# One ramp for three masks, two merged first loads and a new start of the instruction lists, in an attention and SwiGLU kernel

## The chip, the cores and the metric

The kernel runs on one core of a Trainium2 chip. The metric is the device time of one execution in microseconds (us); three runs of the kernel before are shown, and one profiled execution. Engines are named as the profile names them: PE is TensorE (PEld its weight loads), DVE is VectorE, ACT is ScalarE, POOL is GpSimd, SP is SyncE.

## The reference

Attention with 16 extra "beacon" keys for each head, then a SwiGLU feed-forward block over all 4608 tokens (8 batches of 576). There are 8 heads of 64, d_model is 512 and d_ff 1536.

```python
k_all = np.concatenate([beacon_k, k], axis=2)        # 16 + 576 keys
v_all = np.concatenate([beacon_v, v], axis=2)
scores = scale * np.matmul(q, k_all.transpose(0, 1, 3, 2))
scores = np.where(causal, -1000000000.0, scores)     # the beacons are always seen
a = exp(scores - max); a /= a.sum(-1, keepdims=True) + 1e-09
x = np.matmul(a, v_all), heads side by side: 4608 x 512
g = x @ w_gate
out = (g * (1 / (1 + np.exp(-g))) * (x @ w_val)) @ w_out
```

## The kernel before, in words

**Attention.** Heads are worked in pairs (m = 0 to 3), one on the upper and one on the lower 64 rows of PE. The scores of a pair are cut into four units, A to D (`UNITS`); batch 0 runs them in the order of `FIRST_UNITS`: A0 A1 A2 A3, then B0 C0 D0, B1 C1 D1 and so on. A unit takes one PSUM slot of two banks, four slots in all (`take`, `give`). `scores` writes it, `exponent` (ACT, line 414) turns it into bf16 probabilities, `pv` multiplies with the values, `normalize` (DVE) divides. A causal diagonal is masked in one of two ways: in PE, with matmuls that add `ident` times `below` (line 404, plan letter `s`), or after the exponent, by DVE with `upper` (line 423) or by an `affine_select` on POOL (line 427).

**Queries and keys of batch 0** are loaded with their rows on partitions (`runs`, line 216), rows 0 to 255 of each head first (`FRONT`), the rest later. PE transposes them in five turns (`turn`): turn 0 is head pair 0 and turn 1 pair 1 and turn 2 pairs 2 and 3 for the first rows; turn 3 is pairs 0 and 1 and turn 4 pairs 2 and 3 for the rest. `turned_copy` (plan letters K and Q on DVE, k and q on ACT) copies each result to `kT` and `qT`. The first rows of heads 0 and 1 come through `first`, on the SP and ACT queues; all other loads are issued by POOL. Batches 1 and 2 are re-ordered by `pair_up` into `side` first, on DVE or POOL, and then turned (turn 5 is batch 1, pair 0).

**Feed-forward.** `gate_value` (letters G and H) makes 18 units for chunk 0 (units of 240 and 272 tokens, then of 512), later 12 for each chunk of 512 tokens; unit n needs columns 128 f to 128 f + 127 of both weights, `wg` and `wv`, which come in five parts each (g0 to g4, u0 to u4 in the list of loads; f = 3 to 5 is in part 2). `tanh` (ACT), `act1` and `act2` (DVE) follow, then `project` (F) and `evacuate` (O on DVE, o on ACT), which copies a bank of 128 tokens to SBUF and stores it.

**Order.** Nothing is scheduled by a tool: `plan` is a string with one letter for each step, and each engine runs its part of it in that order. `order_of_loads` lists the loads that letters L and l issue; at most eight POOL transfers are under way, a ninth waits for the first of them. Waits between engines are placed by the framework wherever two instructions touch the same tile; `apart` declares that two do not conflict, and is used where two banks of one PSUM tile are handled by different engines:

```python
ins = copy(eng, o_sb[:, cols], ps[:, at, cols])
apart(ins, copied.get((key, 1 - at), []))
```

The last 256 tokens are projected in two parts of 320 and 192 columns, each in a bank of its own (`PARTS`), so that part 0 is copied out beside the matmuls of part 1. `warm` and `keep_warm` (letter h) are matmuls without a use, in places where PE waits.

Of the kernel before, what the change touches and what calls it, by code (L numbers as in the profile page):

```python
# [85 lines left out]
def kernel(  # L86
# [591 lines left out]
    nc.vector.memset(pt[2][:, 0, 0:TOK], 0.0)  # L678
    nc.vector.memset(ident[:], 0.0)
    nc.vector.memset(below[:], 0.0)  # L680
    nc.vector.memset(upper[:], 1.0)
# [7 lines left out]
    def select_below():  # L689
        for row in range(2):  # L690
            r = slice(HALF * row, HALF * row + HALF)
            nc.gpsimd.affine_select(  # L692
                out=below[r], in_=below[r], compare_op=ALU.is_ge, fill=-30000.0, base=0,
                pattern=[[HALF, 2], [-1, P]], channel_multiplier=1,
            )

    def select_upper():
        nc.gpsimd.affine_select(
            out=upper[:], in_=upper[:], compare_op=ALU.is_ge, fill=0.0, base=0, pattern=[[1, P + NB]],
            channel_multiplier=-1,  # L700
        )
# [12 lines left out]
    for b in range(1, NPE):  # L714
        nc.vector.memset(beacons[b][:], 0.0)
    for i in range(NPT):
        nc.vector.memset(pt[i][:, :, 1664:P_W], 0.0)
    for i in range(2):
# [3 lines left out]


# [30 lines left out]
    def piece(kind):  # L754
# [17 lines left out]
        elif kind == "B":  # L772
            select_below()
        elif kind == "U":
            select_upper()
# [57 lines left out]
    ll2ltGHal1G2lGHHa1aatlt21tGH1H2lattF2aGFH112FF2FFGSaEFlHt1GFFaHa2Gltl1t2GtlH12latH12Fa12FFGGtDHS
    ltlaE1FHFFaG2lSFHtl12allF12GFElMFllFHaSG1FEFHaGFFolMHl2l1G2aSOF1H2FaE1FtFG2sHFEaFslF1FDFlSE2FDFE
    DFSESlPpFFFRlDFFFlStFESSDFFEFFsEDFOPEpMPEOpSFFlFRMStRFEFEFSsFEMEFFDFFPplFSFFFFFlFRDSSEFEtFtSFDFF
    FFFEEFlVFFsoOElFFSFtFFDFtSMPEDEtSFElpSDRFFMFFtlMPtESSFEEpRFttFFGFDDSEGHFGa12HHlla1aG21FHl2aGlFHl
    1a2GSHD1ool2aDtPlEGM1ltp2HRlla1GtlSlGH2alEGHG1l2FaM1HHF2a1GFa2HS1FF2FSFFaEFSFEF12lFSPEFpDMFEFSlS
    RFFlEFFtSFttEFFDFSFVFFESEtFFFMsMDEFFFDFEsOFSFFolPttDEFDFSpFFEMFsESFRFFFEFFtFPMEGGOtHoSEtaplHRPtl
    a11Gpt2HD2tGMRaGSt1HH2tGEa1al2G1HSa2GEH1a2GttHGa12SHH1a2MEG1GaM2DSHHES12FaEFFFFF1FDla2FFPSF1FE2F
    pRFFSFFSEFSFESFFFFVEFSFFFFDDFEFFEFFDSoFPFFMlFpFEStlFERFFFFFSSDoEPMFFEFFFDDOMGpoRSElPHGa1S2pHEaR1  # L840
    G2sHlGGEDaHaD12GG1Ha2H12aG1Ha2HaGG12S1EHlHGa2a1D2MSH1FEl2GSMFa1H2EMPaFDF1FSF2EDFFFpSFEFFsRFFFSFF
    FSEFPEEFFSFpERFFSFFFMDVFMSFFDEEPFFDSoFFFFpFFFFEFDOFSPRFDFSpEGFFFEGRGDDFHaO1oHH2aa12P1GpRHGGH2VaG
    Ha1a12HG2Ga1H122HGa1Ga2G1HHH2aa1a21G21GH2aG12HaHGFFFF1a2FFGF1H2aHaGF1H2FaF1GF2F1GHHFFFaa2FF12G1G
    HaFFFFH12F2FFFFFFaG1FHFFoFaFoFF212GGFHaFF1FHFF2FFaFGFFFFOHoG12GHHFaa12GFaFFF1FFF21FHF2GGFFaHFaFF
    1FFF12FHa2FG1GFHF2HFaF1FoaFFoFFFFFG2FF1FFHFaF1FGFF2HGFFFaFF12FH2FFaFFFFF1FFFFF2oFFFFFFFFFFFFOFFF
    FFFFOFoFFFFFFFFFFFOoFFFFFFOo
# [43 lines left out]
```

## Time and profile before

| what | value |
|---|---|
| three runs | 363.02, 363.58, 364.44 us (median 363.58) |
| the profiled execution | 364.1 us, of which the span is 362.1 us |
| TensorE | 352.4 us busy, 97% of the span |
| VectorE, ScalarE, GpSimd | 223.8, 188.9, 124.8 us busy |
| granted TensorE clock | 1.00 throughout |

The span runs from the first to the last instruction; 2.0 us of the profiled execution lie outside it. An engine's busy time leaves out waits, register and semaphore instructions. A time in a row is counted from the start of the span.

### The profile page before, as it was taken

How to read it: one execution, taken by the hardware profiler on the slowest of the kernel's cores; microseconds unless marked ns; L12 is line 12 of the kernel's file. 1: busy time of each engine (PE TensorE's matmuls, PEld its weight loads, DVE VectorE, ACT ScalarE, POOL GpSimd, SP SyncE). 2: the span in 40 equal slices, each digit the busy share in tenths (PEclk: the TensorE clock that was granted, in tenths of full speed). 3: DMA queues.
4: the chain of work that ended last, by engine and by line, in shares of the span. 5: the costliest groups of instructions: out<-in, count | busy, mean ns of one | idle time of the engine just before them, and what ended most of it. 6: DMA issues, size and time to landing. Idle time of an engine off the chain costs nothing.

```text
span 362.1 us, 11881 instructions
## 1 busy us (share of the span) xinstructions
PE 352.4 (97%) x5160; PEld 199.0 (55%) x5160; DVE 223.8 (62%) x437; ACT 188.9 (52%) x286; POOL 124.8 (34%) x188
## 2 busy tenths in 40 slices
PE   7789999999999999999999999999999999999996
PEld 3577566654444565544565556545655554455554
DVE  5576987667765753487518763777467764464341
ACT  4965999832425677543864466546633332331311
POOL 8953589936337545285423013112000000000000
PEclk9999999999999999999999999999999999999999
DMA  9999999999999999999979829602423000110113
GB/s 120 151 179 204 198 184 156 161 170 177 156 134 126 135 142 117 167 143 156 116 121 175 103 34 141 92 0 21 101 83 67 2 2 0 61 60 1 61 58 118
DMA packets 146132, 39.74 MB, mean 110 GB/s; under 512 B 131488, under 2 KB 141728, under 8 KB 146080
## 3 DMA queue, kind: packets, MB, share of 16 engines
q0 software_dynamic: 97424, 19.00, 70.3%
q1 hardware_dynamic: 48368, 19.76, 28.3%
q8 instruction: 40, 0.66, 0.8%
q10 hardware_dynamic: 288, 0.23, 0.2%
q14 instruction: 12, 0.10, 0.1%
HBM read 38.27 MB, written 9.44 MB: 132 GB/s over the span
## 4 chain that ended last, share of the span: by engine, by line
PE 88%; DMA 6%; POOL 2%; DVE 1%; issue 1%; ACT 0%; POOLq 0%
PE gv_ps L174 50%; PE o_ps L174 25%; PE s_ps L174 6%; PE pv_ps L174 4%; PE pv_ps L505 3%; DMA qk<-in_q_dram 3%; DMA wv<-in_moe_w_val_dram 3%; POOL qk L216 1%; PE t_ps L172 0%; DVE u L596 0%; POOL wv L255 0%; POOL wg L255 0%; DVE hT L603 0%; POOL vb L226 0%; POOL below L692 0%
## 5 line engine op out<-in xcount | busy, mean ns | idle before, releaser
L174 PE MATMUL gv_ps<-xT,wv 64*128 64x512 bf16 (+2 forms) x912 | 203.2, 365 | 1.0 <-DMA wv<-in_moe_w_val_dram 1.0
L174 PE MATMUL gv_ps<-xT,wg 64*128 64x512 bf16 (+2 forms) x912 | 203.0, 365 | 0.1
L591 ACT ACTIVATE th<-gv_ps 128x512 f32<-128x512 f32 (+2 forms) x114 | 65.4, 575 | 118.6 <-PE gv_ps L174 118.2
L414 ACT ACTIVATE p<-s_ps 128x832 bf16<-128x832 f32 (+2 forms) x127 | 104.5, 868 | 33.7 <-PE s_ps L174 28.1
L596 DVE SCALAR_TENSOR_TENSOR u<-th,gv_ps 128x512 f32<-128x512 f32 (+2 forms) x114 | 74.7, 656 | 67.4 <-ACT th L591 66.7
L174 PE MATMUL o_ps<-wo,hT 64*128 64x512 bf16 (+2 forms) x912 | 115.8, 365 | 0.0
L174 PEld LDWEIGHTS <-wg 64*128 64x128 bf16 x912 | 82.4, 94 | 45.7 <-PE gv_ps L174 2.4
L174 PEld LDWEIGHTS <-wv 64*128 64x128 bf16 x912 | 81.7, 94 | 41.7 <-DMA wv<-in_moe_w_val_dram 1.1
L603 DVE SCALAR_TENSOR_TENSOR hT<-gv_ps,u 128x512 bf16<-128x512 f32 (+2 forms) x114 | 74.7, 661 | 3.0
L174 PEld LDWEIGHTS <-hT 64*128 64x128 bf16 x912 | 43.0, 94 | 32.5 <-DVE hT L603 0.7
L226 POOL DMA_DIRECT2D vb<-in_v_dram x40 | 34.0, 855 | 63.6 <-PE s_ps L174 25.4
L174 PE MATMUL s_ps<-qT,kT 64*128 64x336 bf16 (+3 forms) x512 | 42.8, 250 | 1.7 <-ACT kT L263 1.0
L174 PEld LDWEIGHTS <-kT 64*128 64x128 bf16 x512 | 23.8, 94 | 22.4 <-ACT kT L263 1.4
L423 DVE TENSOR_TENSOR p<-p,upper 128x256 bf16<-128x256 bf16 (+2 forms) x84 | 23.8, 314 | 11.4 <-ACT p L414 9.9
L226 POOL DMA_DIRECT2D qk<-in_q_dram x25 | 21.2, 852 | 26.3 <-PE gv_ps L174 7.4
L534 DVE TENSOR_TENSOR x<-pv_ps,rec 128x640 bf16<-128x640 f32 (+1 forms) x32 | 25.3, 791 | 1.2
L533 DVE RECIPROCAL rec<-pv_ps 128x10 f32<-128x10 f32 (+1 forms) x32 | 6.8, 212 | 28.1 <-PE pv_ps L174 22.8
L226 POOL DMA_DIRECT2D qk<-in_k_dram x25 | 21.3, 855 | 5.5 <-PE gv_ps L174 4.4
L427 POOL TENSOR_SCALAR_AFFINE_SELECT p<-p 128x256 bf16<-128x256 bf16 (+2 forms) x46 | 17.5, 402 | 13.2 <-ACT p L414 13.0
L264 DVE COPY o_sb<-o_ps 128x512 f32<-128x512 f32 (+2 forms) x18 | 11.6, 657 | 16.2 <-PE o_ps L174 16.1
L174 PEld LDWEIGHTS <-p 64*128 64x128 bf16 x960 | 18.7, 94 | 4.5 <-PE pv_ps L174 0.2
L174 PE MATMUL pv_ps<-vb,p 64*128 64x65 bf16 x960 | 19.9, 189 | 0.0
(65 smaller groups left out, 142.7 us busy)
## 6 DMA issues: line engine op xcount, KB each, us to landing
out_dram<-o_sb SPq DMA_DIRECT2D x34, 256.0 KB, 3.1
vb<-in_v_dram POOLq DMA_DIRECT2D x24, 128.0 KB, 5.9
qk<-in_q_dram POOLq DMA_DIRECT2D x21, 128.0 KB, 5.7
qk<-in_k_dram POOLq DMA_DIRECT2D x16, 128.0 KB, 5.8
wo<-in_moe_w_out_dram POOLq DMA_DIRECT2D x2, 768.0 KB, 10.2
wg<-in_moe_w_gate_dram POOLq DMA_DIRECT2D x3, 384.0 KB, 16.1
wv<-in_moe_w_val_dram POOLq DMA_DIRECT2D x3, 384.0 KB, 15.0
qk<-in_k_dram POOLq DMA_DIRECT2D x2, 576.0 KB, 11.8
```

Of the source, the lines that this page charges most:

```text
L174: ins = nc.tensor.matmul(o, lhsT=l, rhs=r, start=start, stop=stop)
L226: return nc.gpsimd.dma_start(dst[p0 : p0 + n, c, :, 0:D], src[b, :, r : r + n, :].rearrange("h j d -> j h d"))
L264: return eng.tensor_copy(o, i)
L414: nc.scalar.activation(p_of(b, m, u == "A")[:, :, c0 : c0 + w], ps[:, :, 0:w], ACT.Exp, scale=0.125)
L423: nc.vector.tensor_tensor(out=ap, in0=ap, in1=upper[:, None, d : d + w].to_broadcast([P, 2, w]), op=ALU.mult)
L427: nc.gpsimd.affine_select(out=ap, in_=ap, compare_op=ALU.is_ge, fill=0.0, base=d, pattern=[[0, 2], [1, w]], channel_multiplier=-1,)
L505: ins = nc.tensor.matmul(o_ps[:, side, 68 * c : 68 * c + D + 1], lhsT=pt[n % NPT][:, side, col : col + P], rhs=vb[b % 2][:, t, 2 * m + sid ...
L533: nc.vector.reciprocal(rec[:, :, c0:NKT], o[:, :, :, D : D + 1])
L534: nc.vector.tensor_tensor(out=xs[b][:, c0:NKT, P * m : P * m + P].rearrange("p c (h d) -> p h c d", d=D), in0=o[:, :, :, 0:D], in1=rec[:, ...
L591: nc.scalar.activation(th[:, 0:w], gvs[n][:, 0, 0:w], ACT.Tanh, scale=0.5)
L596: nc.vector.scalar_tensor_tensor(out=u[:, 0:w], in0=ths[n][:, 0:w], scalar=1.0, in1=gvs[n][:, 0, 0:w], op0=ALU.add, op1=ALU.mult)
L603: nc.vector.scalar_tensor_tensor(out=hTs[j][:, f, c0:c1], in0=gvs.pop(n)[:, 1, 0 : c1 - c0], scalar=0.5, in1=ths.pop(n)[:, 0 : c1 - c0], o ...
```

## The change

**Constants.** `ident`, `below` and `upper`, each made by a memset and a GpSimd `affine_select`, give way to one tile `ramp` of 128 x 256 ones and zeros from one select. `upper` is a slice of it; `ident` is the difference of two slices and `against` is `ident` times -30000, both made by DVE. The mask matmuls now multiply `against` with a slice of `ramp`, as many and of the same shapes as before.

**First loads.** The first rows of heads 2 to 7 come in one transfer for k and one for q, instead of two each (heads 2 and 3, heads 4 to 7).

**Lists.** `order_of_loads` is new for its first 40 entries or so, `plan` for its first 411 letters of 1758 (before: 409 of 1756; the rest is the same). Turn 4 moves from behind unit D1 to behind unit B0. In the new part DVE takes nine more of the copies out of PSUM and ACT nine fewer; POOL makes 7 of the 8 `side` copies (before 5) and 11 of the masks (before 8). The memsets for batches 1 and 2 move behind the first unit (letter c). The idle matmuls of `keep_warm` become one of 128 rows by 256 columns for each h, 13 of them, instead of two of 64 by 128 for each of 10.

**Output copies.** `apart` is no longer called in `project` and `evacuate`, so the framework places waits between the two banks of an output tile.

```diff
     def keep_warm(ps):
         while heat:
             heat.pop()
-            for row in range(2):
-                r = slice(HALF * row, HALF * row + HALF)
-                nc.tensor.matmul(ps[:, row, 0:P], lhsT=ident[r, :], rhs=ident[r, :], start=True, stop=True)
+            wide = ident[:, None, :].to_broadcast([P, 2, P])
+            nc.tensor.matmul(ps[:, 0, 0 : 2 * P], lhsT=ident[:], rhs=wide, start=True, stop=True)
...
-    below = static.tile([P, 2, P], BF16, name="below")
-    upper = static.tile([P, P + NB], BF16, name="upper")
+    against = static.tile([P, P], BF16, name="against")
+    ramp = static.tile([P, 2 * P], BF16, name="ramp")
+    upper = ramp[:, HALF + 1 : HALF + 1 + P + NB]
...
+                    past = HALF * (1 + hh - g)
                     halves(
                         ("s", n), hh, hh, ps[:, hh, col : col + w],
-                        below[r, g, :], ident[r, HALF * hh + at : HALF * hh + at + w],
+                        ramp[r, past : past + P], against[r, HALF * hh + at : HALF * hh + at + w],
...
-                ins = halves(
+                halves(
...
-                if at:
-                    apart(ins, copied.get((key, 0), []))
...
-        ins = copy(eng, o_sb[:, cols], ps[:, at, cols])
-        apart(ins, copied.get((key, 1 - at), []))
-        copied[key, at] = [ins]
+        copy(eng, o_sb[:, cols], ps[:, at, cols])
...
+    nc.vector.memset(pt[2][:, 0, 0:TOK], 0.0)
+    nc.vector.memset(ramp[:], 1.0)
     nc.vector.memset(beacons[0][:], 0.0)
...
-    for h0, h1 in ((2, 4), (4, H)):
+    for h0, h1 in ((2, H),):
         runs(0, k, h0, h1, 0, FRONT)
         runs(0, q, h0, h1, 0, FRONT)
-    make_identity(nc, ident, nomemset=True)
...
+    nc.gpsimd.affine_select(
+        out=ramp[:], in_=ramp[:], compare_op=ALU.is_ge, fill=0.0, base=-HALF - 1, pattern=[[1, 2 * P]],
+        channel_multiplier=-1,
+    )
...
+    at = HALF + 1
+    nc.vector.tensor_tensor(out=ident[:], in0=ramp[:, at : at + P], in1=ramp[:, at - 1 : at - 1 + P], op=ALU.subtract)
+    nc.vector.tensor_scalar(out=against[:], in0=ident[:], scalar1=-30000.0, scalar2=None, op0=ALU.mult)
...
-    K0.0 Q0.0 v0.2 Q0.4 K0.4 v0.1 v0.0 v0.3 v0.4 v0.5 g1 u0 g0 u1 g2 u2 K1 Q1 b1 u3 g3 g4 u4 Q2 v1.5 K2 v1.3 v1.2
+    Q0.0 K0.0 v0.0 Q0.4 K0.4 v0.2 v0.1 v0.3 v0.4 v0.5 g0 u0 g1 u1 u2 g2 Q1 K1 b1 u3 g3 u4 g4 b2 K2 Q2 v1.3 v1.2
...
-    0LhbTqLLhhWKeBhTQsLTLEKLsqLkELhhSLTQsKELKEsLssUQEshsEhDELshEEELLhLTQZkNZsNSPpJEEILsJPLLERIpSXLDR
+    0LbTWQKAhhhhscLETLQkThsTQKQhSEELLLhsKEhhsDKETsQQEsLLKhsELLEZLNsLhZsENPEsphSRhPsEEEpXJLiYJLDSIPpR
```

**Where instructions stand now.** Three places. The first is POOL's queue at its start. In it `qk` is the tile of loaded queries and keys (64 x heads x elements), `vb` that of values. Before:

```order
L216 DMA qk_101<-in_k_dram 64x2x256
L216 DMA qk_101<-in_q_dram 64x2x256
L216 DMA qk_101<-in_k_dram 64x4x256
L216 DMA qk_101<-in_q_dram 64x4x256
masks.py:199 ISA
masks.py:199 AFFINE_SELECT ident<-ident 128x128
L216 DMA qk_101<-in_k_dram 64x4x320
L216 DMA qk_101<-in_q_dram 64x4x320
L226 DMA vb_103<-in_v_dram 128x8x64
L692 AFFINE_SELECT below<-below 64x256 x2
L216 DMA qk_101<-in_q_dram 64x4x320
L216 DMA qk_101<-in_k_dram 64x4x320
```

and now:

```order
L214 DMA qk_101<-in_k_dram 64x6x256
L214 DMA qk_101<-in_q_dram 64x6x256
L679 ISA
L679 AFFINE_SELECT ramp<-ramp 128x256
L214 DMA qk_101<-in_q_dram 64x4x320
L214 DMA qk_101<-in_k_dram 64x4x320
L224 DMA vb_103<-in_beacon_v_dram 16x8x64
L214 DMA qk_101<-in_q_dram 64x4x320
L214 DMA qk_101<-in_k_dram 64x4x320
L224 DMA vb_103<-in_v_dram 128x8x64
```

Two loads and two selects are gone from ahead of the loads of the remaining rows (64x4x320), and no load of 128 rows of values stands among these any more.

The second is ACT from the copy of the first rows of heads 0 and 1 on: `p` are probabilities (the exponents of units A0, A1, A2 and A3 come first), `t_ps` a result of a turn. Before:

```order
L263 ACTIVATE qk_101<-first 128x256
L263 ACTIVATE qT_105<-t_ps 128x256
L263 ACTIVATE kT_107<-t_ps 128x4x16
L414 ACTIVATE p_109<-s_ps 128x2x368
L263 ACTIVATE qT_105<-t_ps 128x2x256
L263 ACTIVATE kT_107<-t_ps 128x2x256
L414 ACTIVATE p_110<-s_ps 128x2x368
L414 ACTIVATE p_111<-s_ps 128x2x368
L414 ACTIVATE p_first<-s_ps 128x736
```

and now:

```order
L261 ACTIVATE qk_101<-first 128x256
L413 ACTIVATE p_109<-s_ps 128x2x368
L261 ACTIVATE kT_107<-t_ps 128x256
L413 ACTIVATE p_110<-s_ps 128x2x368
L413 ACTIVATE p_111<-s_ps 128x2x368
L413 ACTIVATE p_first<-s_ps 128x736
L413 ACTIVATE p_109<-s_ps 128x2x416
```

Four copies out of `t_ps` left ACT for DVE, and the copy of `kT` for heads 2 and 3 now stands between the first two exponents.

The third is PE near its end, from the last matmuls of part 0 to the first of part 1 (`o_ps` is the output tile; the semaphores waited for are in brackets). Before:

```order
L174 MATMUL o_ps<-wo,hT 128x320
L174 LDWEIGHTS hT
L174 MATMUL o_ps<-wo,hT 128x320
L174 LDWEIGHTS hT [waits PE_49]
L174 MATMUL o_ps<-wo,hT 128x192
L174 LDWEIGHTS hT [waits PE_49]
L174 MATMUL o_ps<-wo,hT 128x192
```

and now:

```order
L173 MATMUL o_ps<-wo,hT 128x320
L173 LDWEIGHTS hT
L173 MATMUL o_ps<-wo,hT 128x320
L173 LDWEIGHTS hT [waits PE_49]
L173 MATMUL o_ps<-wo,hT 128x192 [waits DVE_49]
L173 LDWEIGHTS hT [waits PE_49]
L173 MATMUL o_ps<-wo,hT 128x192 [waits Activation_49]
```

The first matmul of part 1 in each of the two output tiles now waits for DVE or ACT, which copy part 0 of the same tile.

## Rows read from the trace of the kernel before

**Rows 1.** The page's head and part 1: busy time and share of each engine.

```profile
span 362.1 us, 11881 instructions
...
PE 352.4 (97%) x5160; PEld 199.0 (55%) x5160; DVE 223.8 (62%) x437; ACT 188.9 (52%) x286; POOL 124.8 (34%) x188
```

**Rows 2.** Busy time by stretch: from:to, length, engines' busy time, granted clock, DMA.

```profile
20.00:25.00 5.00, 5.00 (x105) 4.08 (x102) 3.50 (x12) 4.05 (x9) 2.08 (x3) 1.00 1.27 184
25.00:30.00 5.00, 3.98 (x75) 3.22 (x73) 2.71 (x8) 1.57 (x5) 0.74 (x1) 1.00 1.22 208
```

**Rows 3.** The chain that ended last, 0 to 30 us: start, length, what.

```profile
7.21 6.64 DMA qk<-in_q_dram
...
17.08 9.92 DMA wv<-in_moe_w_val_dram
```

**Rows 4.** GpSimd in order of time: start, length, instruction, idle before it.

```profile
1.33 0.71 POOL L216 DMA_DIRECT2D qk<-in_k_dram  x1 [0.81 <-POOLq L874]
...
3.93 0.34 POOL masks.py:199 TENSOR_SCALAR_AFFINE_SELECT ident<-ident 128x128 bf16<-128x128 bf16 x1
...
5.38 0.98 POOL L226 DMA_DIRECT2D vb<-in_v_dram  x1
6.30 0.96 POOL L692 TENSOR_SCALAR_AFFINE_SELECT below<-below 64x256 bf16<-64x256 bf16 x2
...
7.83 0.63 POOL L216 DMA_DIRECT2D qk<-in_k_dram  x1
...
14.14 0.76 POOL L255 DMA_DIRECT2D wv<-in_moe_w_val_dram  x1 [0.69 <-DMA qk<-in_q_dram]
```

**Rows 5.** TensorE in order of time, 5 to 35 us.

```profile
5.49 0.32 PE L172 MATMUL t_ps<-ident,qk 64*64 64x64 bf16 x16
...
7.32 0.28 PE L174 MATMUL s_ps<-ident,below 64*128 64x48 bf16 x7 [0.28 <-POOL below L692]
...
14.40 0.51 PE L172 MATMUL t_ps<-ident,qk 64*64 64x64 bf16 x40 [0.46 <-DMA qk<-in_k_dram]
...
21.52 0.26 PE L174 MATMUL gv_ps<-xT,wg 64*128 64x240 bf16 x1
...
27.05 0.27 PE L174 MATMUL gv_ps<-xT,wv 64*128 64x240 bf16 x1 [0.96 <-DMA wv<-in_moe_w_val_dram]
...
34.02 0.44 PE L172 MATMUL t_ps<-ident,side 64*128 64x64 bf16 x18 [0.26 <-POOL side L264]
```

**Rows 6.** ScalarE in order of time, the first 25 us.

```profile
7.64 0.78 ACT L414 ACTIVATE p<-s_ps 128x736 bf16<-128x736 f32 x1 [1.23 <-PE s_ps L174]
...
8.79 0.60 ACT L263 ACTIVATE kT<-t_ps 128x512 bf16<-128x512 bf16 x1
...
11.72 4.80 ACT L414 ACTIVATE p<-s_ps 128x832 bf16<-128x832 f32 x6
...
17.47 2.46 ACT L414 ACTIVATE p<-s_ps 128x832 bf16<-128x832 f32 x3 [0.35 <-PE s_ps L174]
```

**Rows 7.** VectorE in order of time, the first 15 us.

```profile
5.38 0.41 DVE L277 CAST beacons<-first_beacons 16x512 bf16<-16x512 f32 x1 [0.42 <-DMA first_beacons<-in_beacon_k_dram]
...
6.79 0.41 DVE L264 COPY kT<-t_ps 128x256 bf16<-128x256 bf16 x1
...
10.88 0.88 DVE L264 COPY kT<-t_ps 128x320 bf16<-128x320 bf16 x2
...
14.98 0.82 DVE L264 COPY qT<-t_ps 128x640 bf16<-128x640 bf16 x1 [1.02 <-PE t_ps L172]
```

**Rows 8.** All engines in order of time, the last copies.

```profile
357.68 0.49 DVE L264 COPY o_sb<-o_ps 128x320 f32<-128x320 f32 x1 [1.92 <-PE o_ps L174]
...
358.67 0.36 DVE L264 COPY o_sb<-o_ps 128x192 f32<-128x192 f32 x1 [0.50 <-PE o_ps L174]
```

**Rows 9.** All engines in order of time, one pair of output copies.

```profile
186.68 0.60 ACT L263 ACTIVATE o_sb<-o_ps 128x512 f32<-128x512 f32 x1
186.68 0.69 DVE L264 COPY o_sb<-o_ps 128x512 f32<-128x512 f32 x1 [1.49 <-PE o_ps L174]
```

More of the change, by code (lines that the diff above doesn't have):

```diff
@@ L7 @@
 from concourse._compat import with_exitstack
-from concourse.masks import make_identity
 ACT = mybir.ActivationFunctionType
@@ L677 @@
     )
[L678 to L681, printed above, removed]
     nc.scalar.activation(pt[1][:, 0, 0:1], pt[2][:, 0, 0:1], ACT.Exp)
-    for h0, h1 in ((2, 4), (4, H)):
+    for h0, h1 in ((2, H),):
         runs(0, k, h0, h1, 0, FRONT)
         runs(0, q, h0, h1, 0, FRONT)
-    make_identity(nc, ident, nomemset=True)
[L689 to L701, printed above, removed]
+    nc.gpsimd.affine_select(
+        out=ramp[:], in_=ramp[:], compare_op=ALU.is_ge, fill=0.0, base=-HALF - 1, pattern=[[1, 2 * P]],
+        channel_multiplier=-1,
+    )
     idle = take("idle", [P, 2, 512], FP32, "idle_ps")
@@ L713, with constants @@
     give("idle")
[L714 to L718, printed above, removed]
+    def constants(i):
+        if i:
+            for b in range(1, NPE):
+                nc.vector.memset(beacons[b][:], 0.0)
         nc.vector.memset(vb[i][:, :, :, D : D + 1], 1.0)
@@ L721 @@
         nc.vector.memset(kT[i][:, :, NB + S : KPAD], 0.0)
+    for i in range(NPT):
+        nc.vector.memset(pt[i][:, :, 1664:P_W], 0.0)
+    constants(0)
+    at = HALF + 1
+    nc.vector.tensor_tensor(out=ident[:], in0=ramp[:, at : at + P], in1=ramp[:, at - 1 : at - 1 + P], op=ALU.subtract)
+    nc.vector.tensor_scalar(out=against[:], in0=ident[:], scalar1=-30000.0, scalar2=None, op0=ALU.mult)
     done = {}
@@ L771, in piece @@
             pair_up(n, nc.vector if kind == "g" else nc.gpsimd)
[L772 to L775, printed above, removed]
+        elif kind == "c":
+            constants(1)
         elif kind == "T":
@@ L833 @@
[L833 to L846, printed above, removed]
+    0LbTWQKAhhhhscLETLQkThsTQKQhSEELLLhsKEhhsDKETsQQEsLLKhsELLEZLNsLhZsENPEsphSRhPsEEEpXJLiYJLDSIPpR
+    SERGXHELXYDYSaG1LLEGHHLaM2M12PpaLLGG1HR2GLaLX1HY2HGaL1a1GHHallf22G1GHa21HG2a1TH2afq1GaK1S22LllHl
@@ new lines @@
+    ESEaTg1GsHk2EQaG12SlEHTSflaGQkl1SE2lEHSaM1DlEGf2DMsDDHSGEaETqH12lKlDSaE1GTHQkSMf2sPllaEp1SE2sERT
+    sEKPlQlSlfpSElFDFEFFfRDESFDSElPplPpESlFDRFlERSFFFSFEMFTSFEDFQFlFkEFSllEDlMSFFEFFTFFqKFFSFMlSFVED
+    FFloFFlFFFEDFMSMSlOtEFMPplPpERsFDFRFFFEFStlFFEGSGHtFDHDEaGMF1FFaH12POlOpaPp2RlG1GlRHtal2G1HHGVa2
+    1lll2ltGHal1G2lGHHa1aatlt21tGH1H2lattF2aGFH112FF2FFGSaEFlHt1GFFaHa2Gltl1t2GtlH12latH12Fa12FFGGtD
+    HSltlaE1FHFFaG2lSFHtl12allF12GFElMFllFHaSG1FEFHaGFFolMHl2l1G2aSOF1H2FaE1FtFG2sHFEaFslF1FDFlSE2FD
@@ new lines @@
+    FEDFSESlPpFFFRlDFFFlStFESSDFFEFFsEDFOPEpMPEOpSFFlFRMStRFEFEFSsFEMEFFDFFPplFSFFFFFlFRDSSEFEtFtSFD
+    FFFFFEEFlVFFsoOElFFSFtFFDFtSMPEDEtSFElpSDRFFMFFtlMPtESSFEEpRFttFFGFDDSEGHFGa12HHlla1aG21FHl2aGlF
+    Hl1a2GSHD1ool2aDtPlEGM1ltp2HRlla1GtlSlGH2alEGHG1l2FaM1HHF2a1GFa2HS1FF2FSFFaEFSFEF12lFSPEFpDMFEFS
+    lSRFFlEFFtSFttEFFDFSFVFFESEtFFFMsMDEFFFDFEsOFSFFolPttDEFDFSpFFEMFsESFRFFFEFFtFPMEGGOtHoSEtaplHRP
+    tla11Gpt2HD2tGMRaGSt1HH2tGEa1al2G1HSa2GEH1a2GttHGa12SHH1a2MEG1GaM2DSHHES12FaEFFFFF1FDla2FFPSF1FE
@@ new lines @@
+    2FpRFFSFFSEFSFESFFFFVEFSFFFFDDFEFFEFFDSoFPFFMlFpFEStlFERFFFFFSSDoEPMFFEFFFDDOMGpoRSElPHGa1S2pHEa
+    R1G2sHlGGEDaHaD12GG1Ha2H12aG1Ha2HaGG12S1EHlHGa2a1D2MSH1FEl2GSMFa1H2EMPaFDF1FSF2EDFFFpSFEFFsRFFFS
+    FFFSEFPEEFFSFpERFFSFFFMDVFMSFFDEEPFFDSoFFFFpFFFFEFDOFSPRFDFSpEGFFFEGRGDDFHaO1oHH2aa12P1GpRHGGH2V
+    aGHa1a12HG2Ga1H122HGa1Ga2G1HHH2aa1a21G21GH2aG12HaHGFFFF1a2FFGF1H2aHaGF1H2FaF1GF2F1GHHFFFaa2FF12G
+    1GHaFFFFH12F2FFFFFFaG1FHFFoFaFoFF212GGFHaFF1FHFF2FFaFGFFFFOHoG12GHHFaa12GFaFFF1FFF21FHF2GGFFaHFa
@@ L847 @@
+    FF1FFF12FHa2FG1GFHF2HFaF1FoaFFoFFFFFG2FF1FFHFaF1FGFF2HGFFFaFF12FH2FFaFFFFF1FFFFF2oFFFFFFFFFFFFOF
+    FFFFFFOFoFFFFFFFFFFFOoFFFFFFOo
     """
```

17 lines of the change are left out of this document (6 added, 11 removed).

## The prediction

> **What bounds the kernel now.** First the page's head: PE is busy for 352.4 of 362.1 us [rows 1], so 9.7 us at most can come from the waits of PE, and nothing else can be gained without taking work from PE. Then busy time by stretch: from 20 to 25 us PE is busy for 5.00 of 5.00, from 25 to 30 for 3.98 [rows 2]; beyond the first 35 us it hardly waits until the last copies. What there is to gain lies ahead of 35 us. TensorE in order of time shows where [rows 5]: the first gate matmul starts at 21.52, behind batch 0's attention; a wait of 0.96 for a part of `wv` ends at 27.05 (the unit f = 3, the first that needs part 2 of the weights); a wait of 0.26 for a `side` copy ends at 34.02. The chain of waits gives the cause of the second: the load of the remaining query rows of heads 4 to 7, issued at 7.21, takes 6.64, POOL goes on only then, issues part 2 of `wv` at 17.08, and that takes 9.92 [rows 3]. ScalarE sets the pace ahead of 20 us: six exponents in 4.80 from 11.72, three in 2.46 from 17.47, without a gap inside [rows 6].
>
> **POOL's queue.** Four front loads stand from 1.33 to 3.93, and `ident` takes 0.34 behind them [rows 4]. Two loads remain; an issue takes about 0.65 whether it carries two heads (0.71) or four (0.63) [rows 4], so they take 1.3. The ramp's select has 256 columns on 128 partitions, an operation the trace doesn't show: 0.34 is the row for 128 columns, 0.48 each are the two selects of 256 columns on 64 partitions (0.96 together). I take 0.5, the larger. The remaining rows' loads so start at about 3.2 instead of 4.3, 1.1 earlier. `below` (0.96) and `upper` (about the size of `ident`, 0.3) also go from ahead of the weights, which makes 2.4, and the wait of 0.69 for a free transfer [rows 4] should go too: 3.1. The later one of g2 and u2 is issued at about 14.3 instead of 17.08.
>
> When do they land? Two bounds: if the DMA engines had work throughout, only the head start of the first loads counts, 1.1; if each transfer follows its issue, 3.1. A transfer that takes 9.92 where another takes 6.64 [rows 3] stands in a backlog, which speaks for less than 3.1; I take 2.0 from the middle: part 2 is complete at 25.0.
>
> **The front on PE, DVE and ACT.** Unit A0: the beacons' cast ends at 5.79 (5.38 + 0.41), as before, since it waits for its DMA [rows 7]. DVE then makes all three copies, two of 0.41 and a small one of 0.15, to 6.8, where ACT had shared them. PE needs 0.5 for scores and masks, and no longer waits for `below` (0.28) [rows 5]: the first exponent starts at 7.4 instead of 7.64 [rows 6]. Behind it ACT makes one copy of 0.41, only then can PE do unit A1, and ACT waits about 0.5: A1 at 9.1. The two copies of 0.60 for heads 4 to 7 [rows 6] are DVE's now. From here DVE makes the copies of turns 2, 3 and 4: two of about 0.65, four of 0.44, two of 0.82 (rows for 256, 320 and 640 elements [rows 7]), 4.7 with the masks of A2, until 13.9. ACT has exponents alone, 0.74 to 0.82 each (1/2 to 1/6 of its rows [rows 6]): A2 at 10.05, A3 at 10.8, B0 at 11.55, C0 at 12.4, D0 at 13.3, B1 at 14.1, B2 at 16.6 and the end of D2 at 19.2, against 17.47 and 19.93 (17.47 + 2.46). C0 must follow turn 4, which now stands behind B0 on PE, at 11.2; it took 0.51 when it waited for keys until 14.40 [rows 5]. Its last load is issued at about 5.7 instead of 7.83, and without a load of 128 rows of values ahead; with 6.5 from issue to landing, as before (14.35 - 7.83), it lands at 12.2, less 0.9 for the load no longer ahead (its issue took 0.98 [rows 4]) at 11.3. I count no loss, and 1.0 as the bound. Behind D2 come pair 2's value products and one unit's scores, 1.5 as before (21.52 less 19.93): the first gate matmul at 20.7, **0.8 earlier**. Bounds: 1.6 if ACT doesn't wait at A1 and A2, and -0.1 if turn 4 is late by 1.0.
>
> PE then has the same work up to f = 3, and arrives at 26.09 - 0.8 = 25.3, behind the landing at 25.0: the wait of 0.96 goes. **Gain at f = 3: 1.75.** At 34.02 the `side` copy waits for batch 1's rows, which follow part 2 through the same queue and come 2.0 earlier: the 0.26 goes as well. Total 2.0.
>
> **What is costed at nothing.** The mask matmuls are as many and as large as before, and DVE's masks read a slice of `ramp` instead of `upper`. The idle matmuls are 13 of 256 columns, about 0.08 each by the sixteen transposes of 64 columns in 0.32 [rows 5], 1.0 at most, in a front where PE waits longer than that; without that cover they cost the 1.0. DVE's two operations on the ramp end before the first rows land and are cast. More `side` copies on POOL lie ahead of loads that are needed 10 us later.
>
> **The output copies.** With `apart` gone, the matmuls of part 1 of the last tokens wait for the copies of part 0: these start at 357.68 and take 0.49, to 358.17; the next copies follow the last matmul at 358.67 [rows 8], so this group of matmuls takes 1.0 and began at about 357.65. It now begins at 358.2: **a loss of 0.55**, with nothing behind it to hide it. In the other pairs the second bank's copy waits for the first's. In the trace both engines copy at once at 186.68 (0.60 and 0.69) [rows 9]; of the 18 pairs three meet like that, in the others one engine copies both or the times lie apart. In those three ACT is held for 0.69 and a PSUM slot comes back 0.69 later; three other slots are in use meanwhile. Bounds 0 and 2.1; I take 0.2.
>
> The Trainium skill, "PSUM — Partial Sum Buffer", section "PSUM bank collisions raise a hardware error", says that accesses of two engines to different banks run clean. The trace agrees: the two copies at 186.68 run side by side at their usual lengths [rows 9]. So the chip doesn't ask for these waits, but the build has them, in the rows shown for PE; by the page alone the copies would cost nothing, and the sum would be -2.0 instead of -1.25.
>
> **Sum.** -1.75 - 0.26 + 0.55 + 0.2 = -1.25. The span goes to 360.85, the profiled time from 364.1 to 362.85. The median of the runs, 363.58, lies 0.5 below the profiled time; less 1.25 it is **362.3 us**. A measurement of this kernel can tell about 0.5% (1.8 us) from no change, so the likeliest case is within it.
>
> **Rivals.** *B, the front is tighter:* ACT never waits between A0 and D2 and part 2 lands with the larger head start, by 24.4. The first gate matmul gains 1.6, f = 3 gains 2.55, with 0.26 it is 2.8, less 0.75: 361.5 us, or less where the pairs cost nothing. ACT's rows without a gap speak for it [rows 6]; that A1 needs a copy queued behind A0's exponent speaks against it. *C, the transfers were the limit, not their issue:* part 2 comes only 1.1 earlier, and f = 3 starts at 25.95 whatever the front does: -1.1 - 0.26 + 0.75, 363.0 us. The 9.92 of `wv` speaks for it; that POOL stood still for 0.69 and spent 1.3 on selects between the loads speaks against. *D, turn 4 blocks PE's queue, slower:* it runs 3.2 earlier than before in an in-order queue, with C0 and all behind it. If its keys land at 14.35 as before, C0's exponent moves from 12.4 to 15.4, the first gate matmul to 23.7 and f = 3 to 28.3, 1.25 later than before; with the wait at 34.02 gone and 0.75 for the copies 365.3 us, and more if another transfer is late too. It decides from a landing of 12.6 on, where the loss of 1.25 eats the sum. The 6.5 of the row before speaks for it (12.2), the shorter queue ahead against it.
>
> **Chances.** The forecast 0.43 (own range 361.7 to 363.1), B 0.33, C 0.13, D 0.11. B lies past the bound for faster, the forecast and C within it, D at it or beyond: faster 0.34, same 0.55, slower 0.11. The range leaves out D and the far end of B, where both the copies cost nothing and the front gains more than 1.6: 360.8 to 364.4.
>
> **What would show it.** In the changed kernel's trace: the first exponent at 7.4; the load of the remaining rows at 3.2; turn 4 at 11.2 without a wait for DMA; the first gate matmul near 20.7; no wait for `wv` or `wg` ahead of f = 3; two copies of one output tile never at once, and 0.5 of idle PE between the last two groups of matmuls. The prediction is wrong if PE waits for a transfer at turn 3 or turn 4, if ACT has gaps between B0 and D2, if g2 lands behind 25.3, or if the copies' waits show up as idle PE in the middle of the kernel.

## The result: slower by 0.7%

The changed kernel takes 366.57 us (median of 15 runs, 364.96 to 368.26), the kernel before beside it 364.42 (362.72 to 365.34). The ratio is 1.0071, 95% interval 1.0054 to 1.0087, some 2.6 us. Forecast were 362.3 us and a range of 360.8 to 364.4. Of the 4.3 us between forecast and result 0.8 is the base: the forecast started from the 363.58 of three runs, and the kernel before measured 364.42 beside the changed one.

The profiled execution took 368.3 us, span 366.3, more than any other of the 15. So a second execution of the same kernel was profiled (called "again", 366.5 us, span 364.6), and the two are read side by side. The heads of their pages, against [rows 1]; changed kernel first:

```profile
span 366.3 us, 11864 instructions
...
PE 355.4 (97%) x5153; PEld 203.4 (56%) x5153; DVE 228.8 (62%) x441; ACT 185.1 (51%) x276; POOL 126.6 (35%) x189
```

```profile
span 364.6 us, 11864 instructions
...
PE 353.1 (97%) x5153; PEld 202.0 (55%) x5153; DVE 228.7 (63%) x441; ACT 185.2 (51%) x276; POOL 126.7 (35%) x189
```

The head shows no cause. What shows it is the start of the same matmul in two traces: counted from the end, without the idle matmuls, all kernels of this study have the same 5128. Against the trace of before the changed kernel is 0.18 us ahead at the matmul that stood at 33.5 us, 0.19 ahead at 45.0, 2.99 behind at 51.5, then mostly 3.3 to 3.5 behind until the last group, 4.2 behind at its end. In "again" the same places read 1.83 ahead, 1.84 ahead, 1.28 behind, mostly 1.6 to 1.7 behind, 2.5 behind. The start gains in one execution and hardly in the other; 3.1 to 3.2 us are lost between 45 and 51.5, and 0.76 at the end.

**The middle.** Busy time by stretch, before and then after (columns as in [rows 2]: PE, PEld, DVE, ACT, POOL, granted clock, DMA):

```profile
45.00:50.00 5.00, 5.00 (x82) 2.85 (x80) 4.78 (x9) 4.78 (x8) 3.50 (x5) 1.00 2.38 162
50.00:55.00 5.00, 5.00 (x134) 4.08 (x130) 4.18 (x10) 4.45 (x9) 5.00 (x11) 1.00 1.25 207
```

```profile
45.00:50.00 5.00, 3.56 (x58) 1.98 (x55) 4.97 (x8) 3.85 (x7) 4.82 (x9) 1.00 1.68 162
50.00:55.00 5.00, 3.69 (x79) 2.92 (x79) 4.79 (x9) 2.68 (x6) 2.16 (x4) 1.00 1.22 196
```

PE loses 2.75 us of 10. DVE is busy nearly all the time after the change, with one instruction less in each stretch: its instructions have become longer. PE's waits in the changed kernel, 40 to 60 us (total, count, longest), name it:

```profile
PE gv_ps L173 <- DVE hT L602: 1.6, 2, 0.9
PE s_ps L173 <- ACT kT L261: 1.1, 1, 1.1
PE s_ps L173 <- ACT p L413: 0.4, 1, 0.4
```

DVE and then POOL in order of time, changed kernel:

```profile
45.17 1.14 DVE L422 TENSOR_TENSOR p<-p,ramp 128x160 bf16<-128x160 bf16 x1
46.23 0.68 DVE L602 SCALAR_TENSOR_TENSOR hT<-gv_ps,u 128x512 bf16<-128x512 f32 x1
46.83 1.99 DVE L422 TENSOR_TENSOR p<-p,ramp 128x256 bf16<-128x256 bf16 x3
...
50.73 1.47 DVE L422 TENSOR_TENSOR p<-p,ramp 128x224 bf16<-128x224 bf16 x2
```

```profile
45.23 0.76 POOL L426 TENSOR_SCALAR_AFFINE_SELECT p<-p 128x224 bf16<-128x224 bf16 x2
...
46.76 1.16 POOL L262 COPY side<-qk 128x1152 bf16<-128x1152 bf16 x1
47.86 0.82 POOL L426 TENSOR_SCALAR_AFFINE_SELECT p<-p 128x224 bf16<-128x224 bf16 x2
...
50.88 1.17 POOL L262 COPY side<-qk 128x1152 bf16<-128x1152 bf16 x1
```

Each DVE mask here overlaps a copy or a select on POOL and ends behind it: the one at 46.83 at 48.08, POOL's copy at 47.92; the last at 52.20, POOL's copy at 52.05. `hT` at 46.23, which reads PSUM, keeps its 0.68, but the copy overlaps it for only 0.15; over all 17 profiles 15 such `hT` of 512 columns overlap a side copy by 0.1 us or more, and each lasts 0.68 to 0.69. The masks by their line between 40 and 53 us (minimum, median, maximum in ns), before and after:

```profile
L423 DVE TENSOR_TENSOR p<-p,upper x6: 233/273/417, 41.8 to 52.1; 128x256 bf16<-128x256 bf16 x3, 128x224 bf16<-128x224 bf16 x2, 128x160 bf16<-128x160 bf16 x1
```

```profile
L422 DVE TENSOR_TENSOR p<-p,ramp x6: 320/814/1246, 45.2 to 51.0; 128x256 bf16<-128x256 bf16 x3, 128x160 bf16<-128x160 bf16 x2, 128x224 bf16<-128x224 bf16 x1
```

With nothing beside them they take 0.23 us (160 columns), 0.27 (224) and 0.28 (256), in both kernels. Of the six, 3.24 us are beyond that, and PE falls back by 3.18. Call the first number **held**, the second **lag**.

**The front**, PE against [rows 5], changed kernel and then "again":

```profile
12.81 0.19 PE L173 MATMUL s_ps<-against,ramp 64*128 64x64 bf16 x2
14.20 0.21 PE L173 MATMUL s_ps<-against,ramp 64*128 64x64 bf16 x2 [1.20 <-issue]
...
22.59 0.26 PE L173 MATMUL gv_ps<-xT,wg 64*128 64x240 bf16 x1
```

```profile
12.83 0.20 PE L173 MATMUL s_ps<-against,ramp 64*128 64x64 bf16 x2 [0.42 <-issue]
...
20.93 0.26 PE L173 MATMUL gv_ps<-xT,wg 64*128 64x240 bf16 x1
```

PE stops inside one group of mask matmuls of unit C0, without a semaphore ("issue" in the rows). The first gate matmul, 21.52 before, then comes at 22.59 or at 20.93.

**The end**, all engines, against [rows 8]:

```profile
361.14 0.49 DVE L262 COPY o_sb<-o_ps 128x320 f32<-128x320 f32 x1 [1.92 <-PE o_ps L173]
```

```profile
361.69 1.17 PE L173 MATMUL o_ps<-wo,hT 64*128 64x192 bf16 x24 [0.58 <-DVE o_sb L262]
```

The last group waits 0.58 for the copy of part 0, and the next matmul of the second tile for ACT's, as forecast.

### The profile page after: what moved, and what is told of

Its sections match the earlier page's. It is cut to its first block, busy times and chain, and to the rows that moved or that the text cites. A ratio compares the mean times of both kernels' runs of the same rounds, so it can differ in the third digit from the quotient of the medians.

```text
span 366.3 us, 11864 instructions
## 1 busy us (share of the span) xinstructions
PE 355.4 (97%) x5153; PEld 203.4 (56%) x5153; DVE 228.8 (62%) x441; ACT 185.1 (51%) x276; POOL 126.6 (35%) x189
## 4 chain that ended last, share of the span: by engine, by line
PE 90%; DVE 4%; ACT 2%; issue 1%; DMA 1%; POOL 1%; SPq 0%; ACTq 0%
PE gv_ps L173 48%; PE o_ps L173 25%; PE s_ps L173 7%; PE pv_ps L173 4%; PE pv_ps L504 4%; DVE p L422 2%; PE t_ps L171 1%; ACT p L413 1%; DMA first_beacons<-in_beacon_k_dram 1%; DVE u L595 1%; DVE hT L602 1%; PE s_ps L186 1%; ACT th L590 1%; DVE qT L262 0%; POOL side L262 0%
## 5 line engine op out<-in xcount | busy, mean ns | idle before, releaser
L422 DVE TENSOR_TENSOR p<-p,ramp 128x256 bf16<-128x256 bf16 (+2 forms) x80 | 25.7, 353 | 6.3 <-ACT p L413 6.2
L426 POOL TENSOR_SCALAR_AFFINE_SELECT p<-p 128x256 bf16<-128x256 bf16 (+2 forms) x50 | 19.2, 408 | 21.7 <-ACT p L413 21.4
```

Of the source, the lines that this page charges most:

```text
L422: nc.vector.tensor_tensor(out=ap, in0=ap, in1=upper[:, None, d : d + w].to_broadcast([P, 2, w]), op=ALU.mult)
L426: nc.gpsimd.affine_select(out=ap, in_=ap, compare_op=ALU.is_ge, fill=0.0, base=d, pattern=[[0, 2], [1, w]], channel_multiplier=-1,)
```

## The experiments

Theory L: the new middle of the lists lays DVE's masks beside POOL's copies and selects, DVE is held, and in this stretch PE waits for DVE. Rival W: DVE has too much work there, whatever POOL does. Each ratio is to the kernel before, measured beside it, with its 95% interval.

**A second profile** of the changed kernel.

> The changed kernel once more, for a second profile. Theory L (meeting): a mask on DVE that overlaps a copy or select on POOL ends only when that ends; the DVE masks between 44 and 53 us then last 3.2 us longer in all than the same masks alone, and PE's lag behind the kernel before grows by as much in that stretch. In another execution both numbers can differ, but they differ together, within 0.5 us. Rival W (work): DVE has too much work there whatever POOL does; PE's lag then grows by about 3 us there in every execution, whether or not the masks are long.

Held 3.18, lag 3.12, in an execution that ran 1.65 us ahead of the other there. Both theories allow it.

**Masks to POOL.** Units 17, 19, 21, 22, 24 and 28, D to M in the plan:

```diff
-SaM1DlEGf2DMsDDHSGEaETqH12lKlDSaE1GTHQkSMf2sPllaEp1SE2sERTsEKPlQlSlfpSElFDFEFFfRDE
+SaM1MlEGf2MMsMMHSGEaETqH12lKlMSaE1GTHQkSMf2sPllaEp1SE2sERTsEKPlQlSlfpSElFDFEFFfRME
```

> The changed kernel with the six DVE masks of units 17, 19, 21, 22, 24 and 28 (45 to 60 us) made by POOL instead. They take 0.25 us each on DVE when nothing overlaps them, nine instructions, 2.3 us. Theory L: the extension of 3 us goes with them, and PE's lag between 44 and 55 us falls from 3.3 to below 1; the time falls by 2 to 3 us against the changed kernel. Rival W: DVE is relieved of 2.3 us of work alone, of which at most 1.4 lies ahead of 53 us; the time falls by 1.4 at most. A third outcome: POOL is now late with loads and side copies, and the time does not fall.

1.0133 (1.0106 to 1.0160): slower, the third outcome. Held 0, lag 0.15: the loss between 45 and 51.5 is gone, but POOL's masks come too late for the value products behind it, and right behind that wait, from 58.94 to 62.35 us, the granted clock is at the lower level (PE's waits, 40 to 60 us):

```profile
PE pv_ps L504 <- POOL p L426: 2.6, 1, 2.6
```

**Three side copies to DVE, or to ACT.** f to g in the plan (DVE), or to x, a new letter (ACT):

```diff
-SaM1DlEGf2DMsDDHSGEaETqH12lKlDSaE1GTHQkSMf2sPllaEp1SE2sERTsEKPlQlSlfpSElFDFEFFfRDE
+SaM1DlEGg2DMsDDHSGEaETqH12lKlDSaE1GTHQkSMg2sPllaEp1SE2sERTsEKPlQlSlgpSElFDFEFFfRDE
```

> The changed kernel with three of its side copies (the fifth, sixth and seventh; 46.8, 50.9 and 59.8 us on POOL) made by DVE. DVE gets 0.74 us more work for each, POOL loses 1.16. Theory L: the three masks that met these copies are no longer held for 0.95 each, so DVE gains 0.2 each over its new work: within 1 us of the changed kernel, rather faster. Rival W: DVE is the bound and has 1.5 us more to do ahead of 53 us: 1.5 us slower.

1.0036 (1.0014 to 1.0057). Held 0.83, and DVE has two copies of 0.74 more ahead of 54 us: 2.3 together; lag 2.14. DVE was given work and the kernel became 1.3 us faster than the changed one, where W expected 1.5 slower.

> The changed kernel with the fifth, sixth and seventh side copy made by ACT instead of POOL. DVE's own work stays as it was. Theory L (meeting): the masks that met these copies are no longer held, 1.9 us ahead of 54 us; PE's lag grows by about 1.2 us between 44 and 54 us instead of 3.1, and the time falls by 1 to 2 us against the changed kernel, less what ACT's three copies (about 1.1 us each, estimated from 0.65 us for 576 elements) delay its exponents. Theory W (DVE's own work): the lag grows by 3 us as before.

1.0080 (1.0048 to 1.0112): no gain. Held 0.21, and the lag at 51.5 is 1.22, as L expected; the copies (1.16 each) then hold up ACT's exponents:

```profile
PE s_ps L173 <- ACT p L413: 1.4, 2, 0.9
PE o_ps L173 <- ACT p L413: 0.5, 1, 0.5
```

**Halves of the lists.** After letter 192 of the old plan and letter 194 of the new one the same steps are done, but for one load, so the lists can be joined there (about 38 us on PE). `new_start` is the changed kernel with the old rest, `new_middle` the kernel before with the new rest; `order_of_loads` is joined at its 29th entry. `new_start_apart` also has

```diff
+                if at:
+                    apart(ins, copied.get((key, 0), []))
...
-        copy(eng, o_sb[:, cols], ps[:, at, cols])
+        ins = copy(eng, o_sb[:, cols], ps[:, at, cols])
+        apart(ins, copied.get((key, 1 - at), []))
+        copied[key, at] = [ins]
```

> The changed kernel with its lists up to the 194th letter (about 38 us on PE), and behind it the rest of the lists of before (at that letter both plans have done the same steps, but for one load). Theory L (the new middle of the plan lays POOL's copies and selects on DVE's masks, and DVE is the bound there): PE's lead of 0.2 to 2.3 us at 34 us stays, the lag grows by less than 0.7 between 44 and 53 us instead of 3.1, and the end costs 0.75: 1.5 to 2.5 us faster than the changed kernel, 0 to 1.2 below the kernel before. Rival S (the earlier start itself brings POOL and DVE together, whatever the middle): the 3 us are lost here too, as slow as the changed kernel.

> The kernel before with its own start (192 letters), and behind it the changed kernel's list from its 195th letter on; masks, first loads and output copies as before. Theory L: 3 us slower than the kernel before, by masks on DVE that last 3 us longer between 44 and 54 us. Rival S: no loss of more than 1 us.

> As new_start, with the two declarations of independence on the output copies back: 0.8 us faster than new_start by both theories; by theory L 1 to 2 us faster than the kernel before.

`new_start` 1.0018 (1.0004 to 1.0033), 1.9 us better than the changed kernel; `new_middle` 1.0053 (1.0034 to 1.0073), 1.9 us worse than before. The middle makes most of the loss, with either start. Both halves also missed. `new_middle` lost less than the 3 us expected: held 1.79, lag 1.71 in its profile. `new_start` isn't below the kernel before, and its lag is 1.19 where less than 0.7 was expected: a mask at 43.51 meets a load's issue and a side copy of the old middle and lasts 1.53. So rival S holds for a small part: behind the new start the old middle has masks held for 0.39 to 1.47, behind the old start for 0 to 0.13. `new_start_apart` 0.9975 (0.9958 to 0.9992) is the one version clearly below before, by 0.9 us where L expected 1 to 2; it has no wait of PE at all between 40 and 60 us. `best_idle_old` (below), which differs from it in the idle matmuls alone, isn't below before.

**The output copies.** The same lines put back into the changed kernel, and taken out of the kernel before:

> The changed kernel with the two declarations of independence on the output copies back. By the profile of the changed kernel the waits cost 0.75 us at the last group of matmuls and 0.09 at one pair of copies: 0.8 us faster than the changed kernel, with no idle PE between the last two groups. If the waits were hidden, no difference.

> The kernel before without the two declarations of independence on the output copies, and nothing else changed: 0.75 us later from the last group of matmuls on and 0.1 to 0.2 at the pairs of copies, 0.9 slower than before (0.25%). If the waits were hidden: the same time.

1.0060 (1.0036 to 1.0084) against 1.0071, and 1.0015 (0.9996 to 1.0034) against 1: the right sign, neither outside its interval. In every profile with the waits the last matmul falls back by another 0.75 or 0.76; in every one without them by 0. `apart_off` also shows that the old lists can have a loss of their own in the middle: nothing held, yet lag 2.55, with PE waiting for POOL and a transfer (`ramp_late`, with the old lists and nearly as far ahead at 45.0, has none):

```profile
PE t_ps L172 <- POOL side L264: 1.1, 1, 1.1
PE t_ps L172 <- DMA beacons<-in_beacon_k_dram: 0.5, 1, 0.5
```

**Which masks meet POOL's copies.** The cleanest test of L against W, in the changed kernel:

```diff
-SaM1DlEGf2DMsDDHSGEaETqH12lKlDSaE1GTHQkSMf2
+SaD1DlEGf2MDsMMHSGEaETqH12lKlMSaE1GTHQkSMf2
```

> The changed kernel with six masks given back to the engine that made them in the kernel before, in the same order of steps: units 16 and 20 to DVE, units 19, 21, 22 and 24 to POOL. Between 40 and 54 us DVE then makes 5 mask instructions instead of 6 and POOL 6 instead of 5, so either engine has nearly the work of the changed kernel, while POOL's masks can't run beside its own side copies. Theory L (meeting): the DVE masks are held for less than 1.2 us in all instead of 3.2, PE's lag grows by as much and no more between 44 and 54 us, and the time falls by 1.5 to 2.5 us. Theory W (DVE's own work): 0.3 us less work on DVE, the lag still grows by about 2.9 us.

1.0022 (1.0002 to 1.0043), 1.8 us better than the changed kernel, as L expected. Held 1.37 (L expected less than 1.2), lag 1.06; PE's waits from 40 to 60 us, against the 3.1 above:

```profile
PE gv_ps L173 <- DVE hT L602: 0.6, 2, 0.4
PE s_ps L173 <- ACT p L413: 0.4, 1, 0.4
```

W, with a lag of 2.9, falls: DVE had 0.3 us less to do and lost 2.1 less.

> assign_old with the two declarations of independence on the output copies back: 0.75 us faster than assign_old. By theory L 0.5 to 1.5 us faster than the kernel before, as new_start_apart was.

1.0033 (1.0008 to 1.0058): not below before, a miss. The wait at the end is gone in the profile, but the masks were held for 2.00 (lag 1.69), and the stop in the front (below) took 2.15. The clock goes with the miss: the five runs with a mean granted clock of 0.998 or more have a median of 364.01 us, the seven others 366.10. Against `apart_back`, the same exchange of masks is worth 1.0 us here (1.0060 against 1.0033), with intervals that overlap: the sign is that of `assign_old`, the size isn't settled.

**Held and lag in the profiles** (us; masks from 40 to 53 us, lag between the matmuls at 45.0 and 51.5 of before):

| kernel | held | lag | | kernel | held | lag |
|---|---|---|---|---|---|---|
| changed | 3.24 | 3.18 | | new_start_apart | 0.77 | 0.49 |
| again | 3.18 | 3.12 | | split_first | 0.65 | 0.38 |
| apart_back | 3.28 | 3.22 | | best_idle_old | 0.39 | 0.11 |
| assign_old_apart | 2.00 | 1.69 | | ramp_late | 0.01 | 0.10 |
| new_middle | 1.79 | 1.71 | | sides_dve | 0.83 | 2.14 (work added) |
| new_start | 1.47 | 1.19 | | sides_act | 0.21 | 1.22 (work added) |
| assign_old | 1.37 | 1.06 | | apart_off | -0.01 | 2.55 (late transfers) |
| ramp_only | 0.18 | -0.01 | | masks_pool | 0 | 0.15 (no masks on DVE) |

Where no engine was given work and no transfer was late, the lag lies between 0.3 below and 0.1 above the held time (before itself has held 0.13). Over the whole length of all 17 profiles, none of the 592 masks on DVE without a POOL instruction beside it lasts more than 0.01 us longer than alone; of the 60 that overlap a side copy 50 last longer by 0.05 to 1.88. The issue of a load on POOL can hold a mask too: in `assign_old` the one at 45.22 takes 0.60 instead of 0.23 beside issues alone (44.46 to 46.12). That is rarer, 32 masks of 500.

**The stop in the front.** `best_idle_old` is `new_start_apart` with the old idle matmuls:

```diff
-            wide = ident[:, None, :].to_broadcast([P, 2, P])
-            nc.tensor.matmul(ps[:, 0, 0 : 2 * P], lhsT=ident[:], rhs=wide, start=True, stop=True)
+            for row in range(2):
+                r = slice(HALF * row, HALF * row + HALF)
+                nc.tensor.matmul(ps[:, row, 0:P], lhsT=ident[r, :], rhs=ident[r, :], start=True, stop=True)
```

> new_start_apart with the idle matmuls in their old form, two of 64 rows by 128 columns for each. PE stops in the front at its 450th record in all seven kernels with the new start, for 0.1 to 1.2 us, until 1.4 to 1.7 us after the first 16 KB transfer of the instruction queue. Theory F (PE waits for its instructions): nine idle steps ahead of that place now have two matmuls, each with its weight load, so the stop comes at a place of the program 10 to 20 records earlier, and ends again 1.4 to 1.7 us after that transfer. Rival G: the stop belongs to the matmul where it was found (a mask of unit C0), and stays there. The time: within 0.3% of new_start_apart by both.

PE, 12 to 13.5 us:

```profile
13.15 0.22 PE L171 MATMUL t_ps<-ident,qk 64*64 64x64 bf16 x3 [0.97 <-issue]
```

The stop now lies in the transposes of turn 4, ahead of unit C0, and again at the 450th record of PE (matmuls and weight loads counted together), give or take two. F holds, G falls. Nor does the packet only follow PE: in the eleven profiles with the new start and the new idle matmuls the 450th record starts 2.4 to 2.6 us after the packet's start, while the time between that start and any one of the records ahead varies by 1.4 us or more. The time, 1.0015 (0.9993 to 1.0037), is 0.4% above `new_start_apart` (up to 0.9992), more than the 0.3% expected; why is open.

**The first loads and the ramp.**

```diff
-    for h0, h1 in ((2, H),):
+    for h0, h1 in ((2, 4), (4, H)):
```

> new_start_apart with the first rows of heads 2 to 7 in four transfers again: POOL is 1.3 us later with all that follows. If POOL's queue sets the end of the front, as the prediction had it, turn 3, turn 4 or the unit f = 3 waits for DMA and the kernel is 0.5 to 1.3 us slower than new_start_apart; if there is slack, the same within 0.2%.

1.0020 (1.0004 to 1.0037) against 0.9975: 1.6 us slower. But `best_idle_old`, measured beside it with the merged loads, has 1.0015, so the times don't show what the merged loads are worth. In the profile PE waits for transfers at turns 1 and 2 (PE's waits, 5 to 20 us):

```profile
PE t_ps L171 <- DMA qk<-in_k_dram: 1.5, 1, 1.5
...
PE t_ps L171 <- DMA qk<-in_q_dram: 0.4, 1, 0.4
```

That speaks for the merged loads, in one execution, whose granted clock was also at the lower level from 11.86 to 18.69 us.

`ramp_only` is the kernel before with `ramp`, `ident` and `against` made as after the change; `ramp_late` the same, with the later memsets behind the first unit.

> The kernel before with the ramp alone: its lists, four first transfers, idle matmuls and output copies as before. POOL saves two selects of 0.48 and one of 0.3, and the ramp costs 0.1 more than the identity: what POOL issues behind them comes 1.1 us earlier. By the prediction's account the wait of 0.96 for part 2 of the weights goes: 0.5 to 1.0 us faster than before. If transfers, not their issue, set that landing: no change.

> As ramp_only, but the memsets for batches 1 and 2 stand behind the first unit, as in the changed kernel: in ramp_only they stood on DVE behind the two operations that wait for the ramp, and held up the first cast until 6.08 us. By the prediction's account the loads behind the removed selects are issued 1.1 us earlier and the wait of 0.96 for part 2 of the weights goes: 0.5 to 1.0 us faster than before. If transfers, not their issue, set that landing: no change.

`ramp_only` 1.0021 (0.9997 to 1.0046): no verdict on the ramp, since its memsets stood on DVE behind the two operations that wait for the ramp, and the first cast came at 6.08 instead of 4.32. `ramp_late` 0.9991 (0.9974 to 1.0008): the ramp alone can't be told from no change, nor from the 0.5 us that the prediction's account gave it.

## Why the prediction was wrong

**What bounds the kernel: the step that failed first.** The wait of 0.96 for part 2 of the weights and the 0.26 for a side copy [rows 5] were taken as the kernel's. Neither `apart_off` nor `new_middle`, which have the same lists up to 38 us, waits for either. So more than half of the forecast gain, 1.22 of 2.0, was a delay that two of three profiles with the old start don't have; how common it is isn't shown. And the 0.26 didn't go: in both profiles of the changed kernel the same transposes wait 0.25 for POOL's side copy.

**POOL's queue: right.** Two loads, a select of 0.42 (taken 0.5), the remaining rows' first load at 3.20 (3.2), the later of g2 and u2 at 14.81, in "again" 14.17 (14.3), landed at 23.58 and 24.85 (25.0), no wait for weights ahead of f = 3.

**The front on PE, DVE and ACT: right up to unit B0, then not.** In "again" the exponents of A0 to B0 start at 7.77, 9.43, 10.43, 11.11 and 11.78, each 0.2 to 0.4 behind the forecast (in the profiled execution 0.6 to 1.0 behind); C0 comes at 13.08 instead of 12.4, in the profiled execution at 14.45. Turn 4 waits for no transfer. What was missed is the stop at PE's 450th record: in all 12 profiles with the new start it ends 1.4 to 1.7 us after the first packet of 16 KB of an instruction queue, which ends between 10.65 and 13.03. That PE waits there for its instructions is inferred from these times, as no row names the wait. The old start reaches the same record at 13.7 to 14.2 in its three profiles, without such a stop.

At the matmul that stood at 33.5 us the eleven profiles with the new start and merged loads lie between 2.60 ahead and 0.80 behind the trace of before, on average 1.07 ahead; the two others with the old start 0.61 and 1.28 ahead, with before itself 0.63 on average. So the new start gains some 0.4 us instead of 2.0, by means of a few profiles that differ by more than that. By the medians it is -0.25% (`new_start_apart` against before) or +0.07% (`apart_back` against `new_middle`).

The clock in the front goes with this spread. In six of the eleven profiles ("again", `apart_back`, `masks_pool`, `sides_dve`, `new_start`, `sides_act`) the granted clock is recorded at 1.00 from 4.3 to 6.1 us on and doesn't fall in the front; they are 1.14 to 2.60 ahead, 1.82 on average, near the 2.0 forecast. In the five others PE is at the lower level for part of the front (the changed kernel until 10.42, `assign_old` until 9.95, `new_start_apart`, `best_idle_old` and `assign_old_apart` for 3.4 us later on), and they are 0.17 ahead on average. `apart_off` and `new_middle` have 3.4 us at the lower level too, without such a loss, and no run changed the clock alone: its share is argued, not shown. The prediction has no term for the clock. An idle matmul of 256 columns, taken as 0.08, starts 0.11 us after the last at the higher level and 0.21 at the lower.

**What is costed at nothing: the term that turned the sign.** "More `side` copies on POOL lie ahead of loads that are needed 10 us later", put at nothing, asked whom POOL keeps waiting with its queue, not whom it holds while it works; and the first view, PE without idle beyond 35 us, was taken to mean that nothing could be lost there. DVE and ACT were both busy 4.78 of 5 us from 45 to 50 before the change: a stretch with PE full and no reserve beside it. The price is 1.9 us by the medians (both halves of the lists), 3.1 to 3.2 in the profiles of the changed kernel. The trace of before had rows for it: two masks last 1.81 from 61.29 on, the first of them 1.62, where two alone take 0.5, beside a side copy on POOL that ends at 62.75 (DVE, then POOL, in order of time):

```profile
61.29 1.81 DVE L423 TENSOR_TENSOR p<-p,upper 128x256 bf16<-128x256 bf16 x2 [0.59 <-ACT p L414]
```

```profile
61.59 1.16 POOL L264 COPY side<-qk 128x1152 bf16<-128x1152 bf16 x1
```

The Trainium skill, "SBUF — State Buffer", section "Who interferes with whom", states this rule: a DVE instruction with two SBUF inputs contends with a GpSimd instruction that reads SBUF, over a port pair that one of them locks, and the order of issue decides which of the two is blocked. The traces agree for the masks, which read `p` and `ramp` (held 3.24), and for `hT`, which reads one SBUF operand and keeps its 0.68. Whether the second one waits they leave open for the copies: the mask at 61.29 starts 0.3 ahead of POOL's copy and is held all the same, but POOL had been issuing a load from 60.92 to 61.60. No mask in the 17 profiles starts first and meets a copy; of the 49 that start ahead of every select or issue they overlap, none is held. That the number of SBUF operands decides is argued from the rule and the durations; an experiment with a mask of one SBUF input was not tried.

**The output copies: right mechanism, a little small.** 0.55 was taken for the last group, 0.75 measured; 0.2 for the pairs, about 0.1 in the profiles of the changed kernel. Four pairs of before start together, not three (at 186.68, 224.73, 319.64 and 355.06), which puts the upper bound at 2.8 instead of 2.1. Over the four pairs of kernels with and without the waits the medians give 0.11, 0.43, 0.15 and -0.11%, a mean of 0.15%, 0.5 us.

**The rivals.** None was the mechanism. D named the right place, C0 behind turn 4, but a transfer as the cause. No rival looked behind 35 us.

**The sum as measured:** middle +1.9, output copies +0.5, start between -0.9 and +0.2: 1.5 to 2.6 us, beside the 2.6 of the result. What stays open is why the start varies by 3 us between executions of nearly the same program, and how much of it each of three things makes: the clock, the late instruction packet, and late first transfers (the beacons' cast between 5.1 and 6.2 us).

## What to carry to other kernels

A stretch in which PE never waits isn't safe: look how full the engines beside it are, and price each instruction that a new order lays beside another engine's, not only what waits in its queue. When work moves to GpSimd, list what VectorE does at that time with two operands in SBUF. And a wait of 1 us in one profiled execution is no term of a sum until a second execution shows it.
